# Chunk 1's products with wo held until chunk 0's third tile is normalized a second time, and the gate product put at a lower priority, in a planned adaLN, attention and MLP kernel

## The chip, the core and the metric

The kernel runs on one core of one Trainium2 chip. The metric is the device time of one execution in microseconds (us). Before the change the median of three runs is 2027.61 us (2023.54, 2027.61 and 2027.86).

## The reference

Input and output have 2048 rows of 512 numbers. The block is a conditioned attention layer followed by a mixer; `mod` gives three shifts and scales for each half, all of them rows of 512 numbers.

```python
sa, ca, ga, sb, cb, gb = split(silu(c) @ w_mod)
h = layernorm(x) * (1 + ca) + sa
x = x + ga * (attention(h; wqkv, 32 heads of 16) @ wo)
h = layernorm(x) * (1 + cb) + sb
# mixer B(h):
u  = gelu(layernorm(h) @ w1)                    # 512 -> 512
us = four column groups of u, shifted by +1, -1, +2, -2 rows
x1 = h + us @ w2                                # 512 -> 512
h2 = gelu(layernorm(x1) @ w3) @ w4              # 512 -> 1792 -> 512
out = x + gb * (x1 + h2)
```

So each row is normalized three times behind the attention: by the second adaLN layer norm, at the mixer's entry (the kernel's key `xn`), and after the product with w2 (key `xn4`). "Normalized for the second time" in this document means the last of these, `xn4`, the second of the two that the mixer makes.

## The kernel before

**Stages.** A prologue makes q, k and v. Then the attention runs over 4 chunks of 512 query rows and 16 pairs of heads. Behind the attention each chunk of 512 rows, four tiles of 128 rows, goes through what the code calls its tail. Chunk 0's tail begins during the last attention steps; those of chunks 1 to 3 begin when the attention is done. Every product in the tail is made of three TensorE matmuls (high by high, high by low, low by high, lines 356, 358 and 360), so that fp32 is kept.

**A chunk's tail.** `tail(ci)` transposes the attention's output of the chunk (`oT`, line 1244 of the helper `transposed`), and then, tile by tile, makes the product with wo (`wo_mm`). Each tile's product is followed by a chain of work on the other engines: VectorE adds it to x (line 1402), takes the statistics (lines 367, 368 and 1350, in the helper `ln_ops`), centres (1411), scales and shifts (1414) and takes the statistics again; GpSimd makes the inverse root (line 1353, and 1357 and 1358 for the shift); ScalarE applies the normalization (`xn`, line 1364). Two tiles at a time are then transposed by TensorE (`norm_T`, line 1244), split into high and low parts by ScalarE and VectorE (lines 350 and 346, tile name A), and multiplied with w1; the gelu takes ScalarE, VectorE and GpSimd (lines 1452 to 1456). Then comes the product with w2, tile by tile, with its own chain: VectorE adds (line 1507) and takes statistics, GpSimd and ScalarE normalize (`xn4`), and two more steps form the part of the output that does not go through w3: VectorE multiplies by 2 gb in place (line 1512, "the product with the gate") and GpSimd adds it into x1 (line 1513), after which the mark `("z", t)` is set. Chunk 0's w2 stage covers three tiles (its fourth needs rows of chunk 1), and the transposes of `xn4` of the three stand in one group.

**The rest of a chunk.** `rest(ci)` then makes the products with w3, the gelu and the products with w4, in seven pairs of 256 columns for chunk 0. Its weights are split on the way for chunk 0: a DMA brings a raw half (tile name raw), for w4 GpSimd multiplies it by the gate (line 1207), ScalarE makes the high part (1208), VectorE the low part (1209), and a DMA stores the split piece (Ws) for the later chunks. All other weights come back from Ws through a ring of buffers (DMA wr<-Ws, issued by SyncE at line 132); a buffer is loaded again only when the product that used it has been issued.

**What sets the order.** The order of the instructions on each engine is fixed when the program is built, by a planner (`Sched`). TensorE's work comes from generators. A generator yields a condition or a cost; `one()` goes through the list of generators and advances the first whose condition holds. Work on VectorE, ScalarE and GpSimd is put into chains (`sch.chain`), each a list of (engine, planned cost, function) with a ready time and a priority, 1 unless it is given. `misc` emits the chain step that can start first by the planner's clocks; among steps that could start at the same planned time, the chain that stands first in the list wins, and the list is sorted by priority, low numbers first. A step without an engine (None) is run by the planner itself, such as a mark.

Of the kernel before, what the change touches and what calls it, by code (L numbers as in the profile page):

```python
# [71 lines left out]
LNPC = 1  # L72
W0G = 1
WSPL = 1
NLOW = 1
CLOW = 1150
OUTW = 7000.0
# [241 lines left out]
def cD(n=CH):  # L319
    return n / 0.96 + 69  # L320


def cG(n=CH):
    return 2.2 * n + 40
# [3 lines left out]
def kernel(ctx, tc, A_x, A_wqkv, A_wo, B_w1, B_w2, B_w3, B_w4, c, w_mod, out):  # L328
# [951 lines left out]
    def tail(ci):  # L1280
# [91 lines left out]
        def normed(key, t, rs):  # L1372
            tag = xtag(key, t)
            xlive[tag] = xlive.get(tag, 0) + 1
            x = xn[key, t] = (tp if tag == "x4" else fa).tile([P, D], F32, name="xn", tag=tag, bufs=XN[tag])
            y = xbt[t]
            return ln_apply(x, y, rs), mark((key, t))
# [6 lines left out]
        def xn_room(key, t):  # L1384
            return xlive.get(xtag(key, t), 0) < XN[xtag(key, t)]
# [6 lines left out]
            xlive[xtag(key, ts[0])] -= len(ts)  # L1392

        for i, t in enumerate(new):
            yield lambda: sch.room() and xn_room("xn", t) and t in x1t and sch.now() >= arr.get(("x1", t), 0.0) and (ci < 2 or ("z", t - 2 * TPC) in done)
            yield from wo_mm(i, range(KT))
            b = banks.pop(i)
            x1 = x1t[t]
            xb = xbt[t] = pool_of(ci).tile([P, D], F32, name="xb", tag="xb", bufs=XBF if pool_of(ci) is fa else XBT)

            def x1_add(x1=x1, b=b):
                dve.tensor_tensor(x1, x1, b, op=OP.add)
                sch.free(b)

            r, m, ops = ln_ops(x1, True)
            r2, ops2 = ln_ops(xb)

            def center(xb=xb, x1=x1, m=m, ops=ops):
                ops[0][2]()
                sch.late = sch.put("G", 464, sch.T["D"] - cD() + XX, ops[1][2]) + XX  # L1410
                dve.scalar_tensor_tensor(xb, x1, m[:, 0:1], cbrow, op0=OP.subtract, op1=OP.mult)

            def scale(xb=xb, r=r):
                dve.scalar_tensor_tensor(xb, xb, r[:, 0:1], sbrow, op0=OP.mult, op1=OP.add)

            go = partial(sch.chain, ("D", cD(), x1_add), ("D", 2 * cD() + 150, center), ("D", cD(), scale), *ops2,
                         *normed("xn", t, r2), bank=b)
            go()
            if i % 2:
                spawn(norm_T(grp[i // 2], "xn", i // 2), ("T", ci, i // 2))  # L1420
# [77 lines left out]
        for si, ts in enumerate(sub):  # L1498
            yield lambda: all(("g", ci, i, n) in done for i in range(1 + (t0 + 1 in ts)) for n in range(4))
            for t in ts:  # L1500
                yield lambda: sch.room() and xn_room("xn4", t)
                b = dbank("w2")
                yield from rows_mm(b, lambda k, p: g[:, k, p, 130 + (t - t0) * P - SH[k]:][:, :P], w, range(KT), KT)
                xb, x1 = xbt[t], x1t[t]

                def xb_add(xb=xb, b=b):
                    dve.tensor_tensor(xb, xb, b, op=OP.add)
                    sch.free(b)

                r, ops = ln_ops(xb)  # L1510
                sch.chain(("D", cD(), xb_add), *ops, *normed("xn4", t, r),
                          ("D", cD(), lambda xb=xb: dve.scalar_tensor_tensor(xb, xb, 2.0, gbrow, op0=OP.mult, op1=OP.mult)),
                          ("G", cG(), lambda xb=xb, x1=x1: pool.tensor_tensor(x1, x1, xb, op=OP.add)),
                          mark(("z", t)), bank=b)
            spawn(norm_T(ts, "xn4", si), ("T4", ci, si))
        more()
        done.add(("w2", ci))
# [209 lines left out]
```

## Time and profile before

| what | value |
|---|---|
| median of the three runs | 2027.61 us |
| the profiled execution's own time | 2030.02 us |
| span of the profiled execution, first to last instruction | 2028.2 us |
| mean granted TensorE clock | 0.987 |
| first w2 product of chunk 0 | at 1550.15 us of the span |

A row of the profile's windows gives a stretch of the span, its length, the busy time of each engine in it (with the number of instructions), the mean clock that TensorE was granted, the busy share of the DMA engines and the bytes moved. A row of the timeline gives start, duration, engine, source line, operation, what is written from what, and a count where several instructions are merged; a bracket behind it tells how long the engine had been idle and which instruction ended that. All times are of one execution and count from the span's start. Lines are those of the kernel before.

### The profile page before, as it was taken

The page shows a single profiled execution, that of the slowest core. Times are in us where ns is not written, and L with a number is a line of the kernel's source. Part 1 is how long each engine was busy: PE and PEld are TensorE (multiplying, and loading weights), DVE is VectorE, ACT ScalarE, POOL GpSimd, SP SyncE. Part 2 cuts the span into 40 slices and gives each one's busy share as a digit, 9 for nine tenths or more (in the row PEclk, how much of TensorE's full clock was granted, in tenths as well). Part 3 has the DMA queues.
Part 4 walks back from the last instruction along what each step waited for, and adds up shares of the span by engine and source line. Part 5 has one row for each costly group of instructions (what it writes and reads, how often), then busy time and mean ns, then how long its engine had stood idle before and what let it go on. Part 6 is the DMA issues. An engine that isn't in the chain of part 4 may idle for free.

```text
span 2028.2 us, 41674 instructions
## 1 busy us (share of the span) xinstructions
PE 1941.1 (96%) x14456; PEld 1168.8 (58%) x14456; DVE 1658.8 (82%) x2979; ACT 1511.4 (75%) x3085; POOL 1569.9 (77%) x1488
## 2 busy tenths in 40 slices
PE   8999999999999999999999999999998889999999
PEld 5755554554444444444444444444447778898998
DVE  6398788879999999999999999999965786556443
ACT  6438887768999989999999999999984554344443
POOL 6349998879999999999999999999994554335222
PEclk9989999999999999999999999999999899999999
DMA  8877666544443435353434343454414677553541
GB/s 302 233 203 183 158 190 165 135 126 118 81 97 81 97 72 106 72 107 72 107 72 98 80 102 76 95 162 93 90 38 146 228 261 274 218 201 122 200 154 68
DMA packets 185508, 278.01 MB, mean 137 GB/s; under 512 B 117104, under 2 KB 127856, under 8 KB 169008
## 3 DMA queue, kind: packets, MB, share of 16 engines
q1 hardware_dynamic: 181792, 267.20, 49.0%
q10 hardware_dynamic: 2304, 4.20, 0.6%
q0 software_dynamic: 1200, 3.93, 0.5%
q8 instruction: 115, 1.88, 0.4%
q14 instruction: 97, 0.79, 0.1%
HBM read 211.81 MB, written 62.91 MB: 135 GB/s over the span
## 4 chain that ended last, share of the span: by engine, by line
PE 61%; DVE 16%; ACT 10%; issue 6%; POOL 4%; DMA 3%; SPq 1%; ACTq 0%; POOLq 0%; DVEq 0%
PE mb L993 13%; DVE mx L989 11%; PE pv L1083 9%; PE sc L1009 8%; ACT pt L1005 7%; PE w L360 6%; PE w L356 6%; PE w L358 6%; PE pv L1080 4%; PE ot L1110 3%; POOL pt L1058 2%; PE xT L1244 1%; DMA wr<-Ws 1%; DMA wst<-in_A_wqkv_dram 1%; SPq L132 1%
## 5 line engine op out<-in xcount | busy, mean ns | idle before, releaser
L989 DVE TENSOR_REDUCE mx<-mb 128x1 f32<-128x512 f32 x2048 | 1250.1, 680 | 74.5 <-PE mb L993 68.6
L1058 POOL TENSOR_SCALAR pt<-pt 128x1024 f16<-128x1024 uint16 x953 | 1248.1, 1365 | 78.7 <-ACT pt L1005 75.7
L1005 ACT ACTIVATE pt<-sc 128x512 int32<-128x512 f32 x2048 | 1061.3, 615 | 125.6 <-PE mb L993 98.0
L993 PE MATMUL mb<-kst,qtl 62*128 62x512 f32 x2048 | 782.7, 462 | 19.9 <-ACT pt L1005 9.9
L1009 PE MATMUL sc<-qtl,kst 64*128 64x512 f32 x2048 | 739.7, 449 | 5.0 <-DVE mx L989 2.5
L993 PEld LDWEIGHTS mb<-kst,qtl 62*128 62x128 f32 x2048 | 360.1, 193 | 232.3 <-ACT pt L1005 159.9
L1009 PEld LDWEIGHTS sc<-qtl,kst 64*128 64x128 f32 x2048 | 337.0, 186 | 186.8 <-DVE mx L989 119.3
L1083 PE MATMUL pv<-pt,vst 128*32 128x512 f16 x4096 | 385.3, 397 | 20.5 <-ACT ac L1100 20.5
L1456 POOL TENSOR_TENSOR g<-sq,g 128x256 fp32r<-128x256 f32 (+1 forms) x124 | 97.2, 787 | 200.6 <-ACT g L1455 187.2
L1080 PE MATMUL pv<-pt,vst 128*32 128x512 f16 (+1 forms) x2048 | 220.8, 389 | 2.5 <-POOL pt L1058 2.4
L1083 PEld LDWEIGHTS <-vst 128*32 128x32 bf16 x4096 | 91.8, 93 | 227.7 <-issue 209.2
L358 PE MATMUL w<-A,wr 128*128 128x256 f32 (+1 forms) x520 | 156.1, 300 | 0.3 <-DVE A L346 0.3
L356 PE MATMUL w<-A,wr 128*128 128x256 f32 (+1 forms) x520 | 155.9, 300 | 0.2 <-ACT A L350 0.2
L360 PE MATMUL w<-A,wr 128*128 128x256 f32 (+1 forms) x520 | 155.8, 300 | 0.0
L1452 ACT ACTIVATE sq<-w 128x256 f32<-128x256 f32 (+1 forms) x130 | 52.3, 402 | 136.0 <-PE w L360 127.2
L356 PE MATMUL w<-wr,g 128*128 128x512 f32 x270 | 106.9, 396 | 2.9 <-DMA wr<-Ws 2.9
L360 PE MATMUL w<-wr,g 128*128 128x512 f32 x270 | 106.5, 394 | 0.9 <-POOL g L1456 0.9
L358 PE MATMUL w<-wr,g 128*128 128x512 f32 x270 | 106.1, 393 | 0.0
L1434 DVE SCALAR_TENSOR_TENSOR sq<-sq,w 128x256 f32<-128x256 f32 (+1 forms) x130 | 58.3, 449 | 57.7 <-ACT sq L1454 57.5
L356 PEld LDWEIGHTS w<-A,wr 128*128 128x128 f32 x520 | 101.7, 196 | 1.6 <-ACT A L350 0.5
L358 PEld LDWEIGHTS w<-A,wr 128*128 128x128 f32 x520 | 101.5, 195 | 1.5 <-DVE A L346 0.5
L360 PEld LDWEIGHTS w<-A,wr 128*128 128x128 f32 x520 | 101.3, 195 | 0.5 <-issue 0.5
(156 smaller groups left out, 2128.5 us busy)
## 6 DMA issues: line engine op xcount, KB each, us to landing
wr<-Ws SPq DMA_DIRECT2D x66, 1024.0 KB, 5.5
vst<-Vs SPq DMA_DIRECT2D x64, 768.0 KB, 5.6
kst<-Ks SPq DMA_DIRECT2D x126, 384.0 KB, 6.2
Ws<-wr SPq DMA_DIRECT2D x14, 1024.0 KB, 6.2
qtl<-Qs SPq DMA_DIRECT2D x128, 96.0 KB, 4.3
Vs<-vt SPq DMA_DIRECT2D x32, 384.0 KB, 4.2
Ks<-qk SPq DMA_DIRECT2D x16, 512.0 KB, 4.2
Qs<-qk SPq DMA_DIRECT2D x16, 512.0 KB, 3.0
```

Source lines behind the costliest of these rows:

```text
L356: te.matmul(o, lh, rh, start=first, stop=False)
L358: te.matmul(o, lh, rl, start=False, stop=False)
L360: te.matmul(o, ll, rh, start=False, stop=last)
L989: end = sch.crit("D", 605, e + PX, lambda: dve.reduce_max(mxs[u][:, j, g, c:c + 1], b, axis=AX.X))
L993: return ready, lambda: te.matmul(b, lhs, kst[u % 3][r, c * CH:(c + 1) * CH], start=True, stop=True), after
L1005: ea = sch.crit("A", 480, e + PX, lambda: act.activation(pt[s][:, j], b, AF.Exp))
L1009: return ready, lambda: te.matmul(b, kst[u % 3][r, kt * P:(kt + 1) * P], qst[u][r], start=True, stop=True), after
L1058: e_low[s] = XP["G"] + sch.crit("G", 1345, ready, lambda: pool.tensor_scalar(o, i, 0.5, 1.0, op0=OP.mult, op1=OP.mult))
L1080: te.matmul(acc[r:r + n, :], v[:, kt + i, c:c + n].bitcast(F16), pt[s + i].bitcast(F16)[:, j, 0::2], start=False, stop=kt == NKT - 2, skip ...
L1083: te.matmul(acc[r:r + 32, :], v[:, kt, r:r + 32], pt[s].bitcast(F16)[:, j, 1::2], start=kt == 0, stop=False, skip_group_check=True)
L1110: te.matmul(b[:, t * n:(t + 1) * n], ac[:, t * P:(t + 1) * P], smat.rearrange("p j d -> p (j d)"), start=True, stop=True)
L1456: ("G", cG(n), lambda: pool.tensor_tensor(lo, sq, hi, op=OP.subtract)), (None, 0, end), bank=b)
```

## The change

Three constants are added, and three places are edited. `HOLD` is 0 and `i < 0` never holds, so for chunk 1 each of the four products with wo waits until the planner has set the mark `("xn4", 2)`, which stands behind the last step of the third tile's second normalization. `NPRIO` is 1, which is the priority that the chain had. The two steps of the gate are no longer at the end of the w2 chain: they become a chain of their own, put into the list when the normalization is planned as done, with priority 2 and without a bank of PSUM. The arithmetic is the same.

```diff
+ZPRIO = 2
+NPRIO = 1
+HOLD = 0
...
         for i, t in enumerate(new):
+            yield lambda: ci != 1 or i < HOLD or ("xn4", 2) in done
             yield lambda: sch.room() and xn_room("xn", t) and t in x1t and ...
             yield from wo_mm(i, range(KT))
...
                 r, ops = ln_ops(xb)
+                z = (("D", cD(), lambda xb=xb: dve.scalar_tensor_tensor(xb, xb, 2.0, gbrow, op0=OP.mult, op1=OP.mult)),
+                     ("G", cG(), lambda xb=xb, x1=x1: pool.tensor_tensor(x1, x1, xb, op=OP.add)), mark(("z", t)))
                 sch.chain(("D", cD(), xb_add), *ops, *normed("xn4", t, r),
-                          ("D", cD(), lambda xb=xb: dve.scalar_tensor_tensor(xb, xb, 2.0, gbrow, op0=OP.mult, op1=OP.mult)),
-                          ("G", cG(), lambda xb=xb, x1=x1: pool.tensor_tensor(x1, x1, xb, op=OP.add)),
-                          mark(("z", t)), bank=b)
+                          (None, 0, lambda z=z: sch.chain(*z, prio=ZPRIO)), bank=b, prio=NPRIO)
```

In the changed program every line from 75 on stands three further down, and from the held loop on four further down (1402 becomes 1406, 1507 becomes 1511), except that the gate's two steps, 1512 and 1513, become 1515 and 1516. TensorE, VectorE and GpSimd execute the same matmuls and element-wise steps in another order between chunk 0's first product with w2 and the transposes of chunk 1's second normalization; from those on, TensorE's list is the same in both.

TensorE, at chunk 0's first product with w2 (w_24911 is the PSUM bank of tile 0's w2 product, g the gelu's output). Before, nine of its twelve matmuls are followed by chunk 1's products with wo:

```order
L356 MATMUL w_24911<-wr,g_24623 128x512
L358 MATMUL w_24911<-wr,g_24623 128x512
L360 MATMUL w_24911<-wr,g_24623 128x512
L356 MATMUL wo<-wr,A 128x512
L358 MATMUL wo<-wr,A 128x512
L360 MATMUL wo<-wr,A 128x512
```

Three tiles of wo stand there, 36 matmuls, and then the remaining 27 of w2, with the transposes of chunk 1's first two tiles in between. In the changed program the 36 matmuls of w2 stand in one piece, and at their end (w_24957 is the third tile's bank) TensorE's list reads:

```order
L359 MATMUL w_24957<-wr,g_24623 128x512
L361 MATMUL w_24957<-wr,g_24623 128x512
L363 MATMUL w_24957<-wr,g_24623 128x512
L1247 MATMUL xT<-ident,xn 128x128 x12
L359 MATMUL wo<-wr,A 128x512
L361 MATMUL wo<-wr,A 128x512
L363 MATMUL wo<-wr,A 128x512
```

So the twelve transposes of chunk 0's three tiles now stand directly behind the third tile's product, and three tiles of wo behind them; these are followed by 27 matmuls of w3 and then the transposes of chunk 1's first two tiles.

VectorE, from the split of chunk 1's attention output on (A). Before, chunk 1's chain takes the next place, with the first w2 tile's addition 15 rows on:

```order
L346 TENSOR_TENSOR A<-xT,A 128x2x256 x4
L1402 TENSOR_TENSOR x_24869<-x_24869,wo 128x512
L367 BN_STATS tst<-x_24869 128x6
L368 BN_AGGR tmv<-tst 128x2
L1350 TENSOR_SCALAR tmv<-tmv 128x1
L1411 SCALAR_TENSOR_TENSOR xb<-x_24869,tmv,cbrow 128x512
L1414 SCALAR_TENSOR_TENSOR xb<-xb,trs,sbrow 128x512
L1402 TENSOR_TENSOR x_24871<-x_24871,wo 128x512
```

In the changed program the three w2 tiles come first there. L1511 is a w2 tile's addition and L1515 the product with the gate; the rows from tile 1's addition (w_24932) to tile 2's statistics are:

```order
L1511 TENSOR_TENSOR xb<-xb,w_24932 128x512
L370 BN_STATS tst<-xb 128x6
L371 BN_AGGR tmv<-tst 128x2
L1353 TENSOR_SCALAR tmv<-tmv 128x1
L1515 SCALAR_TENSOR_TENSOR xb<-xb,gbrow 128x512
L1511 TENSOR_TENSOR xb<-xb,w_24957 128x512
L370 BN_STATS tst<-xb 128x6
L371 BN_AGGR tmv<-tst 128x2
L1353 TENSOR_SCALAR tmv<-tmv 128x1
```

The first tile's product with the gate thus still stands ahead of the third tile's addition. Then come the other two products with the gate, the low parts of four raw halves and the split of the transposes, and only then chunk 1's first addition (L1406). Further on, chunk 1's second tile (x_24871) goes through these rows on VectorE in the changed program:

```order
L1406 TENSOR_TENSOR x_24871<-x_24871,wo 128x512
L1418 SCALAR_TENSOR_TENSOR xb<-xb,trs,sbrow 128x512
L370 BN_STATS tst<-xb 128x6
L371 BN_AGGR tmv<-tst 128x2
L1353 TENSOR_SCALAR tmv<-tmv 128x1
L370 BN_STATS tst<-x_24871 128x6
L371 BN_AGGR tmv<-tst 128x2
L1353 TENSOR_SCALAR tmv<-tmv 128x1
L1415 SCALAR_TENSOR_TENSOR xb<-x_24871,tmv,cbrow 128x512
L1406 TENSOR_TENSOR x_24873<-x_24873,wo 128x512
L1418 SCALAR_TENSOR_TENSOR xb<-xb,trs,sbrow 128x512
L370 BN_STATS tst<-xb 128x6
```

Its last statistics are now eleven rows behind its addition, with no row of chunk 0 in between.

## The prediction

> **What bounds the kernel now.** I read the page's first part first, then the windows over the stretch that the change reorders, then TensorE's waits there, then the timeline of each engine around those waits.
>
> ```profile
> span 2028.2 us, 41674 instructions
> PE 1941.1 (96%) x14456; PEld 1168.8 (58%) x14456; DVE 1658.8 (82%) x2979; ACT 1511.4 (75%) x3085; POOL 1569.9 (77%) x1488
> ```
>
> TensorE (PE) is busy 96% of the span, so a reordering can only gain what TensorE loses: time in which it has nothing to do, and time at a lower clock. TensorE's list differs from chunk 0's first w2 matmul, at 1550.15 us, to the sixteen transposes of chunk 1's second normalization, at 1677.87. The windows cut this stretch at its waits:
>
> ```profile
> core 0: us, PE busy (x) PEld busy (x) DVE busy (x) ACT busy (x) POOL busy (x), PEclk, DMA share, GB/s
> 1550.15:1677.87 127.72, 110.31 (x567) 97.47 (x565) 103.93 (x190) 61.21 (x122) 71.33 (x92) 0.93 0.63 224
> 1567.00:1590.00 23.00, 13.38 (x75) 11.75 (x73) 19.73 (x41) 11.79 (x21) 14.24 (x25) 0.84 0.61 221
> 1590.00:1639.00 49.00, 46.97 (x260) 42.13 (x260) 37.66 (x73) 24.36 (x52) 27.43 (x37) 0.97 0.62 220
> 1639.00:1651.00 12.00, 6.36 (x25) 5.93 (x25) 10.52 (x17) 6.60 (x13) 9.30 (x10) 0.72 0.61 228
> 1677.87:2028.00 350.13, 341.32 (x2055) 306.80 (x2052) 187.38 (x387) 143.78 (x347) 123.89 (x186) 1.00 0.48 174
> ```
>
> TensorE's idle time in the stretch is 127.72 - 110.31 = 17.4 us. The lower clock costs (1 - 0.84) x 13.38 + (1 - 0.97) x 46.97 + (1 - 0.72) x 6.36 = 2.1 + 1.4 + 1.8 = 5.3 us. So 22.7 us are lost, 1.1% of the span, and 105.0 us are work that stays. Behind the stretch the list does not change, and its 8.8 us of idle stay. VectorE is busy for 103.9 of the 127.7 us, so a shorter stretch leaves it little slack. What ended TensorE's waits in the stretch:
>
> ```profile
> PE xT L1244 <- ACT xn L1364: 15.3, 5, 5.6
> PE w L356 <- DMA wr<-Ws: 2.0, 1, 2.0
> ```
>
> The waits are transposes that wait for ScalarE's normalized tiles, and one load of weights. Here are the transposes that waited, with two matmuls that show the pace behind the third wait:
>
> ```profile
> 1568.89 0.99 PE L1244 MATMUL xT<-ident,xn 128*128 128x128 f32 x7 [1.57 <-ACT xn L1364]
> ...
> 1579.36 2.39 PE L1244 MATMUL xT<-ident,xn 128*128 128x128 f32 x10 [5.58 <-ACT xn L1364]
> ...
> 1589.06 1.57 PE L1244 MATMUL xT<-ident,xn 128*128 128x128 f32 x7 [2.22 <-ACT xn L1364]
> ...
> 1591.07 0.41 PE L358 MATMUL w<-A,wr 128*128 128x256 f32 x1
> 1591.28 0.41 PE L360 MATMUL w<-A,wr 128*128 128x256 f32 x1
> ...
> 1645.59 1.75 PE L1244 MATMUL xT<-ident,xn 128*128 128x128 f32 x7 [5.64 <-ACT xn L1364]
> ```
>
> A wait costs more than itself when the clock falls behind it. Behind the 2.22 us wait two matmuls that are 256 wide start 0.21 us apart; at full clock matmuls twice as wide start 0.23 apart (1611.25 and 1611.48, below). Behind the 1.57 us wait seven transposes take 0.99 us, 0.14 each; behind 5.58, 2.22 and 5.64 they take 0.24, 0.22 and 0.25 each. So the 5.3 us of lost clock belong to these three waits, about 2 us for a long one.
>
> **The change, part by part.** Nothing is added or removed on any engine; the terms are the waits in the new order.
>
> *Removed: the 1.57, 5.58 and 2.22 us waits.* Their transposes move, and with them the clock that followed, 2.1 + 1.4 us.
>
> *First new wait: chunk 0's third tile.* The 36 matmuls of w2 now run in one piece. How VectorE and ScalarE are occupied ahead of the third tile, two rows tell, and how long its normalization takes, the same chain of chunk 1's third w2 tile:
>
> ```profile
> 1552.60 2.57 DVE L346 TENSOR_TENSOR A<-xT,A 128x512 fp32r<-128x512 f32 x4
> ...
> 1570.51 2.19 ACT L1208 ACTIVATE wr<-raw 128x512 fp32r<-128x512 f32 x4
> ...
> 1611.25 0.39 PE L358 MATMUL w<-wr,g 128*128 128x512 f32 x1
> 1611.48 0.39 PE L360 MATMUL w<-wr,g 128*128 128x512 f32 x1
> ...
> 1611.91 0.69 DVE L1507 TENSOR_TENSOR xb<-xb,w 128x512 f32<-128x512 f32 x1
> ...
> 1615.29 0.82 ACT L1364 ACTIVATE xn<-xb,trs 128x512 f32<-128x512 f32 x1 [1.08 <-POOL trs L1358]
> ```
>
> At 0.23 us from start to start the last w2 matmul starts at 1550.15 + 35 x 0.23 = 1558.2 and ends 0.39 later, at 1558.6. From addition to normalized tile it is 1616.1 - 1611.9 = 4.2 us. VectorE splits A until 1555.2; then tile 0 is normalized at 1559.4, and its product with the gate, in the order still ahead of tile 2's addition, reads and overwrites the same tile, so it waits for that. Tile 2's addition starts at 1560.0 and its tile is ready at 1560.0 + 4.2 = 1564.2. ScalarE's four weight halves (2.2 us) stand between tiles 1 and 2 and end at about 1563.5, so they just fit. TensorE waits 1564.2 - 1558.6, about 5.5 us, and the clock costs 2 us behind it. The wo products behind the transposes then cover the split of A. The cover that this wait had before, 36 matmuls of wo, is what the change takes away. Bounds: 4.2 us without the gate's detour, 7 if one more chain gets ahead.
>
> *Second new wait: chunk 1's first two tiles.* From the second tile's product to their transposes TensorE has 12 matmuls of wo (2.7 us) and 27 of w3 (384 wide, so three quarters of 0.23 each: 4.7), 7.4 us. On VectorE the twelve rows shown with the change stand in the way; their groups:
>
> ```profile
> L1209 DVE TENSOR_TENSOR wr<-raw,wr 128x512 fp32r<-128x512 f32 x26 | 25.0, 990 | 0.0
> ...
> L367 DVE BATCH_NORM_STATS2 tst<-xb 128x6 f32<-128x512 f32 x13 | 8.9, 687 | 0.1
> L1434 DVE SCALAR_TENSOR_TENSOR sq<-sq,w 128x384 f32<-128x384 f32 x12 | 6.6, 549 | 3.7 <-ACT sq L1454 3.5
> ...
> L1414 DVE SCALAR_TENSOR_TENSOR xb<-xb,trs,sbrow 128x512 f32<-128x512 f32 x6 | 5.4, 902 | 0.9 <-POOL trs L1353 0.9
> ...
> L1402 DVE TENSOR_TENSOR x<-x,wo 128x512 f32<-128x512 f32 x6 | 4.1, 680 | 0.8 <-PE wo L360 0.8
> ```
>
> Two additions (0.68), two scalings (0.90), three statistics (0.69, with their two small steps about 1.0) and one centring (about an addition) make 6.9 us. Behind them stand the root on GpSimd and the normalization: the 4.2 us of the chain above less its addition and statistics, 2.5 us. 9.4 - 7.4 = 2.0 us. Bounds: 0, and 2.2 with 1.4 of clock, as the nearest such wait had. I take 2.0 without clock.
>
> *Third new wait: chunk 1's last two tiles.* Between the fourth tile's product and its transposes lie 21 matmuls of w4, 24 of w3 and 31 of w1: 4.8 + 4.1 + 3.6 = 12.5 us. From the split of the first two tiles on, VectorE's order holds seven steps of gelu (3.8 at 0.55), five weight halves (5.0 at 0.99), four additions (2.7), two sets of statistics (2.0), and two scalings, a centring and two splits (3.9), 17.4 us. With the terms so far TensorE ends the first two tiles' transposes at about 1582 and stands at the last two's at about 1601. VectorE starts that split at about 1584, since ScalarE has three weight halves ahead of it, and ends at 1601.4; the tile is ready 2.5 us later, near 1604. I take 3.0, with 0.8 of clock; bounds 0 and 5.64 with 2.4, the wait of the same kind at 1645.59.
>
> *Weights.* The second w2 piece loads when w1's first half is done. From the chain of waits:
>
> ```profile
> 1598.07 6.55 DMA wr<-Ws
> 1604.66 0.50 PE w L356
> ```
>
> From issue to use it took 6.6 us. In the new order 24 matmuls of w1 (0.12 each, half of 0.23) and 6 of w2 cover 2.9 + 1.4 = 4.3, so the wait is 2.3 where it was 2.0. The loads of w1's and w2's first pieces are issued later too, behind the last wo, but 11 us or more ahead of their use. SyncE has weight stores ahead of them; these end with the same wo product, so I cost that at nothing; if one of these loads landed late, it would show as a second DMA wait.
>
> *Fourth wait: chunk 2's first two tiles, 5.64 us before.* The last products with wo are followed by nine more w3 matmuls than before (10 instead of 1 in the third w3 pair), 1.6 us. VectorE also has fewer weight halves left there, since pairs 0 and 1 come earlier. I take 1.5, bounds 0 and 5.64; no clock.
>
> *The gate's priority elsewhere.* In chunks 1 to 3 the gate's product moves by a few rows behind the statistics of the next tile. The transposes of those tiles come much later than their normalization (at 1677.87 for chunk 1), so the cost is nothing; the gap to them covers it.
>
> **Sum.** New loss: idle 5.5 + 2.0 + 3.0 + 2.3 + 1.5 = 14.3, clock 2.0 + 0.8 = 2.8, together 17.1 us, against 22.7: 5.6 us less. The profiled execution took 2030.02 us around its span of 2028.2, so its like would take 2024.4. It is 2.4 above the median of the runs, 2027.61; from that, 2022.0 us.
>
> The Trainium skill (TensorE: Matmul & The Clock Gate, section "HAM oscillation — how this bites in real kernels") gives the rule "no PE-idle gaps >~3.4µs", and half the clock for about 3.4 us behind such a gap. That speaks against one gap of 5.5 us and for several short ones. By it the two long waits of before would cost 1.7 us each and only the first new one would, so the gain would be (17.4 + 3.4) - (14.3 + 1.7) = 4.8 us. The trace disagrees on the threshold, since the half pace also followed the 2.22 us wait.
>
> **Rivals.**
> - *All the later waits are covered* (0.12). Only the first one and the weights are left: 5.5 + 2.0 + 2.3 = 9.8, a gain of 12.9, 2014.7 us. For it speaks that 36 wo matmuls and the w3 pairs now lie between chains; against it VectorE's 104 us of work.
> - *The loss only moves* (0.26). The wait at the third tile takes the place of 5.58 us, and the late chains of chunk 1 that of 5.64 us: if the third and fourth wait come to 5 and 4 us, with 2 of clock in one of them, the loss is 5.5 + 2 + 2 + 5 + 2 + 2.3 + 4 = 22.8: 2027.7 us. For it: VectorE is busy for 86 to 88% of the two windows in which TensorE waits longest. Against it: the chain that TensorE waits for first now stands together on VectorE, without another chunk's rows in it.
> - *VectorE's queue becomes the bound* (0.16). Holding wo moves all of chunk 1's additions behind the w2 tiles, among gelu steps and weight halves. If two of the second to fourth waits are like 1645.59 (5.64 + 2.4), the loss is 7.5 + 2.3 + 16.1 + 2.0 = 27.9: 5.2 us slower, 2032.8. Against it: 36 matmuls of wo and the first w3 pairs lie between. It decides from 12.9 us over these three waits on (22.7 - 9.8); I expect 7.3.
>
> **How the numbers follow.** The forecast has 0.46. About 0.2% (4 us) is what a measurement of this kernel can tell from no change. Faster by more: 0.46 + 0.12 = 0.58; within: 0.26; slower: 0.16. The range from 2014 to 2032 takes in the first rival's time and the bounds of the waits, and leaves out most of the last rival.
>
> **What would show it.** Right: in the changed profile TensorE waits once for 5 to 6 us behind w2's third tile for ScalarE, with slow matmuls of wo behind it; the wait ahead of chunk 2's transposes shrinks to under 3 us; and from chunk 1's second normalization on all starts are earlier by the gain. Wrong: waits of 5 us at chunk 1's transposes, a second wait for a load of weights, or a start of the unchanged part that does not move.

## The result, and the profile after

| | before | changed |
|---|---|---|
| median of 12 runs | 2026.53 us | 2019.37 us |
| range | 2023.54 to 2029.34 | 2016.26 to 2022.31 |
| profiled execution, span | 2030.02, 2028.2 us | 2021.44, 2019.7 us |

The ratio is 0.9966 with a 95% interval of 0.9956 to 0.9975: 7.2 us, or 0.34%, faster. The forecast was 2022.0 with a range from 2014 to 2032.

The stretch that the change reorders, from chunk 0's first w2 matmul to the sixteen transposes of chunk 1's second normalization, took 127.6 us before: the prediction ends it at 1677.87, but the transposes start at 1677.71. These are the windows of the changed kernel over the stretch, the piece behind the first waits in which TensorE never stops, and the part behind the stretch (us, then busy time of TensorE, its weight loads, VectorE, ScalarE and GpSimd with their instructions, then TensorE's clock, DMA share and GB/s):

```profile
1549.47:1670.78 121.31, 107.62 (x566) 94.33 (x564) 100.97 (x190) 60.24 (x123) 71.66 (x92) 0.97 0.66 236
1563.87:1570.12 6.25, 6.25 (x20) 5.36 (x21) 3.79 (x6) 2.60 (x5) 3.30 (x3) 0.52 0.98 371
1670.78:2019.70 348.92, 339.84 (x2055) 305.55 (x2053) 187.82 (x387) 143.11 (x347) 125.49 (x186) 1.00 0.47 175
```

And one of the kernel before, behind its stretch:

```profile
1714.00:1720.00 6.00, 5.63 (x35) 5.64 (x36) 3.35 (x7) 3.77 (x10) 0.67 (x2) 0.72 0.02 7
```

The stretch is 6.3 us shorter. TensorE is idle in it for 121.31 - 107.62 = 13.7 us (17.4 before), and its busy time is 2.6 us above the prediction's 105.0 us of work (5.3 before). All of the lower clock lies behind the first waits, (1 - 0.52) x 6.25 = 3.0 us; from there to the end of the stretch the clock is 1.00. That is more than 2.6, because the prediction multiplied the mean clock of windows in which TensorE is partly idle with its busy time, and the mean counts the idle time too. Read in windows of half a microsecond, the lower clock costs 5.8 us before and 3.0 us now, and the work is about 104.5 us. Of the span's 8.5 us the remaining 2.2 lie ahead of the stretch and behind it, where TensorE's list is the same in both; 1.6 of them lie behind it and are busy time, since before the clock fell there once more (0.72 in the window at 1714 us).

TensorE's waits in the stretch, by what ended them (us in all, how many, the longest):

```profile
PE xT L1247 <- ACT xn L1367: 10.5, 6, 2.9
PE w L363 <- POOL g L1460: 2.2, 1, 2.2
PE w L359 <- DMA wr<-Ws: 0.9, 1, 0.9
```

And one by one in TensorE's timeline, with the first three waits at chunk 0's three tiles, the pace of wo behind them, then chunk 1's first two tiles, its last two, the weights, a gelu, and chunk 2's first two tiles:

```profile
1558.70 0.33 PE L1247 MATMUL xT<-ident,xn 128*128 128x128 f32 x1 [0.56 <-ACT xn L1367]
1560.60 0.33 PE L1247 MATMUL xT<-ident,xn 128*128 128x128 f32 x1 [1.57 <-ACT xn L1367]
1563.87 2.40 PE L1247 MATMUL xT<-ident,xn 128*128 128x128 f32 x10 [2.94 <-ACT xn L1367]
...
1567.35 0.63 PE L359 MATMUL wo<-wr,A 128*128 128x512 f32 x1
1567.77 0.63 PE L361 MATMUL wo<-wr,A 128*128 128x512 f32 x1
...
1570.12 0.40 PE L361 MATMUL wo<-wr,A 128*128 128x512 f32 x1
1570.35 0.39 PE L363 MATMUL wo<-wr,A 128*128 128x512 f32 x1
...
1582.53 0.98 PE L1247 MATMUL xT<-ident,xn 128*128 128x128 f32 x7 [1.54 <-ACT xn L1367]
1605.38 0.98 PE L1247 MATMUL xT<-ident,xn 128*128 128x128 f32 x7 [2.52 <-ACT xn L1367]
1617.82 0.50 PE L359 MATMUL w<-wr,g 128*128 128x512 f32 x1 [0.94 <-DMA wr<-Ws]
1652.70 0.50 PE L363 MATMUL w<-wr,g 128*128 128x512 f32 x1 [2.23 <-POOL g L1460]
1659.21 0.98 PE L1247 MATMUL xT<-ident,xn 128*128 128x128 f32 x7 [1.40 <-ACT xn L1367]
```

Three waits with 5.07 us in all stand at chunk 0's tiles. Behind them matmuls of wo start 0.42 us apart, and from 1570.12 on 0.23 apart. No other wait is followed by a slow pace: seven transposes take 0.98 us behind 1.54, 2.52 and 1.40 us, where before they took up to 1.75. The unchanged part starts 6.9 us earlier in the span (1670.78 instead of 1677.71).

One wait is new in kind, the 2.23 us at 1652.70 for the low part of a gelu on GpSimd. GpSimd's timeline around it, with VectorE's step that GpSimd waited for:

```profile
1650.68 0.99 POOL L1356 TENSOR_TENSOR trs<-tmv,mhalf 128x1 f32<-128x1 f32 x1 [6.38 <-DVE tmv L1353]
1651.64 1.00 POOL L1460 TENSOR_TENSOR g<-sq,g 128x384 fp32r<-128x384 f32 x1
...
1650.45 0.15 DVE L1353 TENSOR_SCALAR tmv<-tmv 128x1 f32<-128x1 f32 x1
```

The low part stands in GpSimd's queue behind the root of chunk 2's second tile, and that root waits 6.38 us for its statistics.

### The profile page after: what moved, and what is told of

The parts are those of the page before. It is cut to its first block, busy times and chain, and to the rows that moved or that the text cites. A ratio compares the mean times of both kernels' runs of the same rounds, so it can differ in the third digit from the quotient of the medians.

```text
span 2019.7 us, 41655 instructions
## 1 busy us (share of the span) xinstructions
PE 1934.4 (96%) x14456; PEld 1162.1 (58%) x14456; DVE 1656.3 (82%) x2979; ACT 1510.2 (75%) x3085; POOL 1571.9 (78%) x1488
## 4 chain that ended last, share of the span: by engine, by line
PE 61%; DVE 16%; ACT 9%; issue 6%; POOL 4%; DMA 3%; SPq 0%; ACTq 0%; POOLq 0%; DVEq 0%
PE mb L996 13%; DVE mx L992 12%; PE pv L1086 9%; PE sc L1012 8%; ACT pt L1008 7%; PE w L363 5%; PE w L359 5%; PE w L361 5%; PE pv L1083 4%; PE ot L1113 3%; POOL pt L1061 2%; PE xT L1247 1%; POOL trs L1356 1%; PE v L359 1%; DMA wr<-Ws 1%
## 5 line engine op out<-in xcount | busy, mean ns | idle before, releaser
L361 PE MATMUL w<-A,wr 128*128 128x256 f32 (+1 forms) x520 | 153.4, 295 | 0.3 <-DVE A L349 0.3
L359 PE MATMUL w<-A,wr 128*128 128x256 f32 (+1 forms) x520 | 153.2, 295 | 0.3 <-ACT A L353 0.3
L363 PE MATMUL w<-A,wr 128*128 128x256 f32 (+1 forms) x520 | 153.1, 294 | 0.0
L359 PEld LDWEIGHTS w<-A,wr 128*128 128x128 f32 x520 | 98.7, 190 | 1.7 <-ACT A L353 0.5
L361 PEld LDWEIGHTS w<-A,wr 128*128 128x128 f32 x520 | 98.7, 190 | 1.6 <-DVE A L349 0.5
L363 PEld LDWEIGHTS w<-A,wr 128*128 128x128 f32 x520 | 98.6, 190 | 0.5 <-issue 0.5
```

Of the source, the lines that this page charges most:

```text
L359: te.matmul(o, lh, rh, start=first, stop=False)
L361: te.matmul(o, lh, rl, start=False, stop=False)
L363: te.matmul(o, ll, rh, start=False, stop=last)
```

## The experiments

The **theory**: the gain comes from chains that stand together on VectorE, so that the long waits of before (5.58 and 5.64 us) become one long wait, in three pieces, and several short ones, and only the long one costs the pace. It needs both parts of the change. **Rivals**: one part alone does it; the clock differs by chance from execution to execution; or VectorE has no slack, and what is won at one wait comes back at another.

All edits are to the changed kernel. Added lines shift the line numbers in their profiles. "Stretch" is the same stretch in the one profiled execution; "above" is TensorE's busy time above 105.0 us, the fill taken off (4.09 us for 36, as in a row below); with about 104.5 us of work it is some 0.4 us too low in most rows. Each ratio is to the kernel before, run on the same chip; rows come from four chips, so they are compared by their ratios.

| run | edit | stretch | idle | above | median | ratio (95%) |
|---|---|---|---|---|---|---|
| e5 | none | 120.23 | 12.6 | 2.6 | 2018.95 | 0.9957 (0.9945 to 0.9970) |
| e1 | hold alone | 131.36 | 18.3 | 8.1 | 2028.79 | 1.0010 (0.9997 to 1.0023) |
| e2 | priority alone | 127.35 | 16.6 | 5.7 | 2026.63 | 0.9999 (0.9988 to 1.0011) |
| e3 | fill, twice | 118.82 | 8.7 | 1.0 | 2024.23 | 0.9983 (0.9968 to 0.9997) |
| e6 | fill, once | 118.43 | 8.4 | 1.0 | 2020.01 | 0.9968 (0.9957 to 0.9979) |
| e4 | released earlier | 121.73 | 13.7 | 3.0 | 2022.28 | 0.9979 (0.9966 to 0.9991) |
| e7 | two holds | 130.11 | 16.6 | 8.5 | 2030.56 | 1.0018 (1.0008 to 1.0027) |
| e8 | two holds, at w2 | 131.95 | 19.3 | 7.6 | 2031.85 | 1.0022 (1.0010 to 1.0033) |
| e9 | gate behind | 119.98 | 12.9 | 2.0 | 2019.33 | 0.9973 (0.9962 to 0.9984) |
| e10 | root behind | 124.70 | 14.6 | 5.2 | 2023.82 | 0.9990 (0.9980 to 1.0001) |
| e11 | e9, e10 and fill | 121.90 | 10.4 | 3.1 | 2023.46 | 0.9983 (0.9972 to 0.9995) |
| e12 | all rows behind, fill | 119.85 | 10.2 | 1.0 | 2020.70 | 0.9979 (0.9966 to 0.9992) |

### The changed kernel again (e5)

> The changed kernel once more, on the chip and beside the runs that the next three are compared with. Theory (the gain is in the order, so it comes again): 2019 to 2020 us beside 2026 to 2027 of before, the stretch from the first w2 matmul to the sixteen transposes again 121.3 us. Rival (the gain was one of the clock drops that differ from execution to execution): a stretch that differs by 3 us or more, and a time nearer to before.

The gain came again, 8.5 us by the medians, so it isn't one of the clock's chance drops. The stretch was 120.23 us, 1.1 less than in the first profile, with the same waits in the same places but for the 0.56 us. So one profile each can't tell apart two stretches that differ by about 1 us.

### Each part alone (e1, e2)

For e1 the gate's two steps go back to the end of the chain; for e2 the line with the hold is taken out.

```diff
 sch.chain(("D", cD(), xb_add), *ops, *normed("xn4", t, r),
-          (None, 0, lambda z=z: sch.chain(*z, prio=ZPRIO)), bank=b, prio=NPRIO)
+          ("D", cD(), lambda xb=xb: dve.scalar_tensor_tensor(xb, xb, 2.0, gbrow, op0=OP.mult, op1=OP.mult)),
+          ("G", cG(), lambda xb=xb, x1=x1: pool.tensor_tensor(x1, x1, xb, op=OP.add)),
+          mark(("z", t)), bank=b, prio=NPRIO)
```

```diff
-yield lambda: ci != 1 or i < HOLD or ("xn4", 2) in done
```

> The hold alone, with the gate's two steps back at the end of each w2 chain. Theory (both parts count): on VectorE tile 0's gate product now stands ahead of tile 1's statistics and waits for tile 0's normalized tile, and three weight halves (2.7 us) stand ahead of tile 2's statistics. So tile 2 is normalized about 3.6 us later than in the changed kernel (at about 1567.4 instead of 1563.8), TensorE's wait at the third tile grows from 5.1 to about 8.5 us, and half of the gain of 7.2 us is lost: about 2023 us. Rival A (the hold does all of it, the gate's priority nothing): 2019.4 us as the changed kernel, third-tile wait 5 us. Rival B (the gate's priority does all of it): 2026.5 us as before.

> The gate's lower priority alone, without the hold; TensorE again puts 36 wo matmuls between the w2 tiles. Theory: the waits of before stay, because what made them long is chunk 1's chain between the w2 tiles on VectorE: waits for normalized tiles of 12 to 16 us in the stretch, 2025 to 2027 us in all (before: 15.3 and 2026.5). Rival (the gate's priority does most of it): 2019 to 2021 us and waits of about 10 us.

The timeline with the hold alone: TensorE's waits at chunk 0's tiles and at chunk 2's, and on VectorE the first tile's product with the gate, which now stands ahead of the second tile's statistics:

```profile
1562.80 0.47 PE L1247 MATMUL xT<-ident,xn 128*128 128x128 f32 x1 [4.10 <-ACT xn L1367]
1565.91 2.40 PE L1247 MATMUL xT<-ident,xn 128*128 128x128 f32 x10 [2.64 <-ACT xn L1367]
...
1663.64 1.76 PE L1247 MATMUL xT<-ident,xn 128*128 128x128 f32 x7 [3.60 <-ACT xn L1367]
...
1558.35 0.69 DVE L1516 SCALAR_TENSOR_TENSOR xb<-xb,gbrow 128x512 f32<-128x512 f32 x1 [1.46 <-ACT xn L1367]
```

Its windows over the stretch and at chunk 2's transposes:

```profile
1549.44:1680.80 131.36, 113.08 (x566) 98.79 (x565) 102.80 (x192) 60.99 (x124) 72.22 (x92) 0.91 0.66 227
1663.00:1671.00 8.00, 7.36 (x28) 6.88 (x29) 6.22 (x10) 3.98 (x8) 3.46 (x3) 0.60 0.77 240
```

With the priority alone, the wait at chunk 0's last tiles in the timeline:

```profile
1574.38 2.39 PE L1247 MATMUL xT<-ident,xn 128*128 128x128 f32 x10 [5.58 <-ACT xn L1367]
```

The priority alone keeps the 5.58 us wait to the hundredth and gains nothing in time, as expected. But all waits for normalized tiles sum to 10.8 us, where 12 to 16 were expected: the one at chunk 2's tiles is 2.06 us instead of 5.64. Ahead of these, TensorE now waits 2.31 and 0.93 us for parts of gelus, and the clock falls behind these and behind 2.33 us for weights. The hold alone isn't half the gain but none: the waits at chunk 0's tiles are 7.0 us (8.5 expected), but busy time above the work rises to 8.1 us. The clock falls not only behind these but also behind 3.19 us at chunk 1's last two tiles, behind 2.15 us for weights and at chunk 2's tiles, where the wait is long again (3.60). Rival A falls with e1; rival B, whose time e1 has, falls with e2. Neither part is worth anything alone here. At chunk 0's tiles the rows say why: with the gate's product ahead of the next tile's statistics, VectorE waits 1.46 us for ScalarE in the middle of the chains that the hold has put together. Why the later waits grow again in e1 isn't shown.

### Useless work in the long wait (e3, e6)

The transposes of the identity go into the PSUM bank that the real ones then overwrite. This is e6; e3 lacked the condition on `filled`.

```diff
+NFILL = 36
 b = dbank("xT")
+if n > 2 * P and kk[0] == 0 and not filled:
+    filled.append(1)
+    for _ in range(NFILL):
+        te.transpose(b[:, :P], ident, ident)
```

> The changed kernel with 36 transposes of the identity put ahead of the twelve transposes of chunk 0's three normalized tiles, into the bank that these then overwrite; all other lists are unchanged. The work is useless; it only keeps TensorE busy for 36 x 0.14 = 5.0 us in its wait of 5.1 us. Theory (the slow matmuls behind the wait cost 2.8 to 3.0 us and come from TensorE having been idle): the transposes and the wo matmuls behind run at full pace, wo starts 0.23 us apart, the stretch is 2 to 3 us shorter, 2016.5 to 2017.5 us. Rival A (the slow pace has another cause, or useless transposes don't keep the clock): the same 2019.4 us, or later by up to 0.5 us because the real transposes now queue behind the fill. Rival B (VectorE holds the rest: the 2 to 3 us come back as a longer wait at chunk 1's first two tiles, 1.5 now, 3.5 to 4.5 then): 2019.4 us with a shorter first half.

> As the fill before, but with the 36 useless transposes only at chunk 0's three tiles; the first try issued them a second time in the last chunk, where nothing waits (39 more rows, 4 us). Theory: the profile of the first try had 2.5 us less in the stretch (118.8 instead of 121.3), so without the second fill 2016.5 to 2017.5 us. Rival (the clock that is kept here is lost elsewhere, or the fill costs as much as it keeps): 2019.4 us as the changed kernel.

e3 issued the fill once more in chunk 3, where nothing waits; that row of its timeline, and then e6's windows over the stretch, the wait and a piece behind chunk 1's first two tiles, with the transposes there:

```profile
1906.69 4.09 PE L1248 MATMUL xT<-ident 128*128 128x128 f32 x36
```

```profile
1551.16:1669.59 118.43, 110.08 (x601) 97.53 (x600) 100.36 (x190) 60.12 (x122) 71.36 (x92) 0.99 0.68 245
1560.00:1572.00 12.00, 10.83 (x72) 9.60 (x71) 11.05 (x20) 5.99 (x11) 7.92 (x10) 1.00 0.61 221
1582.05:1585.55 3.50, 3.50 (x15) 3.50 (x14) 3.43 (x8) 3.29 (x8) 2.01 (x2) 0.51 0.00 0
```

```profile
1581.55 1.22 PE L1254 MATMUL xT<-ident,xn 128*128 128x128 f32 x7 [1.89 <-ACT xn L1374]
```

The clock behind the wait is 1.00 where it was 0.52, and in both runs the stretch is 1.4 to 2.9 us shorter than in the two profiles without a fill. So the slow pace behind the first waits does come from TensorE's idling, and it cost 3.0 us. But in both runs the clock then falls behind chunk 1's first two tiles, where it had stayed at 1.00 in the changed kernel: (1 - 0.51) x 3.50 = 1.7 us, behind a wait of only 1.89 us. e6's rival, that the clock kept here is lost elsewhere, held in part. In the total the fill shows no gain (0.9968 against 0.9957 and 0.9966, with intervals that overlap), and both runs miss the 2016.5 to 2017.5 us of their theory; e3 also pays for its second fill.

### Released one tile earlier (e4), and a second hold (e7, e8)

The added lines are those of e4, e7 and e8 in this order:

```diff
-yield lambda: ci != 1 or i < HOLD or ("xn4", 2) in done
+yield lambda: ci != 1 or i < HOLD or ("xn4", 1) in done
+yield lambda: ci != 1 or (("xn4", 1) in done if i < 2 else ("xn", grp[0][1]) in done)
+yield lambda: ci != 1 or (("w2", 0) in done if i < 2 else ("xn", grp[0][1]) in done)
```

> The hold is released one tile earlier, when the second tile's normalization is planned; VectorE's order through the three w2 tiles stays as in the changed kernel, and 12 wo matmuls (2.8 us) now stand in the third-tile wait; 48 w3 matmuls instead of 27 then stand ahead of chunk 1's first two tiles. Theory (the third-tile wait is a real loss that any work can fill): that wait falls from 5.1 to about 2.3 us, the wait at chunk 1's first two tiles from 1.5 to about 0, and the time to about 2015 to 2016 us. Rival (VectorE, 84% busy in the stretch, is the bound, and a wait filled here only comes back later): waits of 13 to 14 us in the stretch as now, 2018 to 2020 us.

With twelve wo matmuls in it, the wait at chunk 0's third tile fell to 2.46 us, as expected. But e4's timeline has a second wait behind it, at chunk 1's first two tiles; below it are GpSimd's rows ahead of that wait:

```profile
1560.24 2.40 PE L1247 MATMUL xT<-ident,xn 128*128 128x128 f32 x10 [2.46 <-ACT xn L1367]
...
1583.69 1.75 PE L1247 MATMUL xT<-ident,xn 128*128 128x128 f32 x7 [6.66 <-ACT xn L1367]
...
1578.62 0.99 POOL L1356 TENSOR_TENSOR trs<-tmv,mhalf 128x1 f32<-128x1 f32 x1 [3.12 <-DVE tmv L1353]
1579.58 1.34 POOL L1210 TENSOR_TENSOR raw<-raw,gbrow 128x512 f32<-128x512 f32 x1
1580.89 0.99 POOL L1356 TENSOR_TENSOR trs<-tmv,mhalf 128x1 f32<-128x1 f32 x1
...
1576.92 0.15 DVE L1353 TENSOR_SCALAR tmv<-tmv 128x1 f32<-128x1 f32 x1
```

The second tile's statistics are ready at 1577.07, but its root stands on GpSimd behind the third tile's, which waits until 1578.6, and behind a raw half, and starts at 1580.89. The stretch and the sum of the waits are as in the changed kernel, as the rival said; the median is above its 2018 to 2020 us. e7 and e8 take the third tile out of the way.

> Chunk 1's first two wo tiles are released one tile earlier (as in the run with the earlier release), and its last two are held until its second tile is normalized. Theory (the 6.7 us wait of the earlier release came from GpSimd's queue: the second tile's root stood behind the third tile's root, which waited for statistics on VectorE): with the third tile out of the way that wait falls to 2 us or less, the third-tile wait of chunk 0 stays at 2.5, and the time is 2014 to 2016 us. Rival (VectorE is the bound; gelu steps and weight halves take the third tile's place and the wait stays at 5 us or more): 2018 to 2021 us.

> As the run before it, but the first two wo tiles are released as soon as chunk 0's last w2 product is issued, so that 16 wo matmuls (3.7 us) stand in the third-tile wait instead of 12. Theory: that wait falls from 5.1 to about 1.4 us with no slow matmuls behind it, the others as in the run before: 2012 to 2015 us. Rival (chunk 1's additions now get ahead of chunk 0's third tile or its split, or VectorE is the bound): waits of 12 us or more in the stretch, 2018 to 2021 us.

e7's timeline has TensorE at a w4 product instead, waiting for its weights, and on GpSimd the raw halves of these weights behind the roots, with the second tile's root behind them:

```profile
1581.67 0.80 PE L361 MATMUL w<-wr,g 128*128 128x512 f32 x1 [5.06 <-ACT wr L1213]
...
1576.18 0.99 POOL L1358 TENSOR_TENSOR trs<-tmv,mhalf 128x1 f32<-128x1 f32 x1 [5.11 <-DVE tmv L1355]
...
1578.19 0.99 POOL L1358 TENSOR_TENSOR trs<-tmv,mhalf 128x1 f32<-128x1 f32 x1
...
1579.68 2.50 POOL L1212 TENSOR_TENSOR raw<-raw,gbrow 128x512 f32<-128x512 f32 x2
...
1583.57 0.99 POOL L1358 TENSOR_TENSOR trs<-tmv,mhalf 128x1 f32<-128x1 f32 x1
```

With w4 now ahead of chunk 1's first two tiles, w4's weights are late by 5.06 us (4.90 in e8). The wait at the two tiles is 1.36 us, but only because TensorE comes to them later: their transposes start 37.5 us after the first w2 matmul, as in e4 (37.6). The second tile's root no longer stands behind the third's, but behind the two raw halves and a gelu's low part: its statistics are ready at 1581.31, and it starts at 1583.57. So these runs don't show that the third tile's root alone made the wait in e4. In e8 the wait at chunk 0's third tile fell to 1.61 us with the transposes at full pace, as expected, but chunk 2's tiles then wait 5.56 us. Both kernels are slower than before, which neither the theories nor the rivals had. What stands behind a root on GpSimd in these rows waits for VectorE's statistics with it.

### The rows between the third tile and its normalization (e9, e12)

In e9 tile 0's product with the gate is emitted behind the third tile's addition; VectorE's list differs in one pair of rows, the others in none. The first diff is e9's, where the gate's steps of tile 0 are kept in `late`. In e12 (the second diff, without the halves) all that stood in the way goes behind: on VectorE the gate's products of tiles 0 and 1, on GpSimd tile 0's addition into x1, on ScalarE four weight halves; 32 transposes fill the wait.

```diff
 def xb_add(xb=xb, b=b, t=t):
     dve.tensor_tensor(xb, xb, b, op=OP.add)
     sch.free(b)
+    if t == 2:
+        while late:
+            late.pop(0)()
+        done.add(("a", 2))
```

```diff
+if (ci, t) == (0, 2):
+    def root(fn=ops[1][2]):
+        fn()
+        done.add("root2")
+        while late:
+            late.pop(0)()
+    ops = ops[0], (*ops[1][:2], root)
+def gate(fn):
+    if ci or "root2" in done:
+        fn()
+    else:
+        late.append(fn)
...
```

> The changed kernel with one pair of rows exchanged on VectorE and nothing else moved on any engine: tile 0's product with the gate now stands behind the third tile's addition instead of ahead of it. Theory: the third tile's addition no longer waits for tile 0's normalization and the gate product (0.9 us in the changed kernel: free at 1558.35, started at 1559.29), so the third tile comes 0.9 us earlier, TensorE's three waits at the tiles sum to 4.1 to 4.2 us instead of 5.1, and the stretch is 0.9 us shorter; in all 2018 to 2018.5 us, which the total alone can't tell from the changed kernel. Rival A: ScalarE's four weight halves, which end at 1562.6, now hold the third tile, and the wait stays at 4.8 us or more. Rival B: the 0.9 us come back at chunk 1's first two tiles (1.5 us becomes 2.4), and the stretch stays at 120.2 to 121.3 us.

> The changed kernel with what stands between the third tile's addition and its normalized tile put behind it: on VectorE the gate products of tiles 0 and 1 (behind the third tile's statistics), on GpSimd the addition of tile 0 into x1 (behind the third tile's root), on ScalarE the four weight halves (behind the third tile's normalization); and 32 useless transposes of the identity (0.11 us each in the run with one fill, 3.5 us) in the wait. Nothing else moves. Theory: addition at 8.7 us from the first w2 matmul, statistics until 10.3, root until 11.5, normalized at 12.4, so that the transposes that wait for the third tile start at 12.4 to 12.6 us instead of 13.9 to 14.4; with the pace kept, the stretch is 1.5 us shorter than with the fill alone (118.4): 116.5 to 117.5 us, and 2015 to 2018 us in all. Rival A (one of the moved rows doesn't matter and another row or the root's own duration holds the tile): the third tile at 13.5 us or later. Rival B (the third tile comes earlier, but chunk 1's tiles on VectorE don't): the waits at chunk 1's tiles grow by the 1.5 us, from 1.9 to 3.4 at the first two, and the stretch stays at 118 us or more.

e9's rows of VectorE, GpSimd and ScalarE for the third tile, from its addition to its normalization:

```profile
1557.17 0.69 DVE L1512 TENSOR_TENSOR xb<-xb,w 128x512 f32<-128x512 f32 x1 [0.18 <-PE w L363]
1557.77 0.69 DVE L1526 SCALAR_TENSOR_TENSOR xb<-xb,gbrow 128x512 f32<-128x512 f32 x1
1558.37 0.69 DVE L370 BATCH_NORM_STATS2 tst<-xb 128x6 f32<-128x512 f32 x1
...
1558.54 1.27 POOL L1527 TENSOR_TENSOR x<-x,xb 128x512 f32<-128x512 f32 x1
1559.77 1.00 POOL L1356 TENSOR_TENSOR trs<-tmv,mhalf 128x1 f32<-128x1 f32 x1
...
1561.66 0.82 ACT L1367 ACTIVATE xn<-xb,trs 128x512 f32<-128x512 f32 x1 [0.23 <-POOL trs L1361]
```

The gate's product only slid between addition and statistics, and the root waits behind a GpSimd addition of 1.27 us. The three waits sum to 4.74 us, no less than e5's 4.51: nearly rival A's 4.8, though GpSimd and not ScalarE holds the tile. In e12, with all three out of the way, the third tile comes 13.0 us after the first w2 matmul (13.9 to 14.4 without the change, 12.4 expected). These are e12's waits there and at chunk 1's first two tiles:

```profile
1560.92 1.31 PE L1264 MATMUL xT<-ident,xn 128*128 128x128 f32 x10 [0.60 <-ACT xn L1384]
1577.68 0.33 PE L1264 MATMUL xT<-ident,xn 128*128 128x128 f32 x1 [2.56 <-ACT xn L1384]
1579.90 1.44 PE L1264 MATMUL xT<-ident,xn 128*128 128x128 f32 x7 [1.89 <-ACT xn L1384]
```

The time won comes back at chunk 1's first two tiles, 4.45 us where the fill alone had 1.89. Rival B held, and the stretch is longer than e6's by 1.4 us. The median, 2020.70 us, misses the theory's 2015 to 2018.

### The new wait on GpSimd (e10), and three edits together (e11)

In e10 the root of chunk 2's second tile is emitted behind the gelu's low part; GpSimd's list differs in one pair of rows. e11 joins e9, e10 and 30 filling transposes.

```diff
-sch.late = sch.put("G", 464, sch.T["D"] - cD() + XX, ops[1][2]) + XX
+sch.late = sch.put("G", 464, sch.T["D"] - cD() + XX, partial(held.append, ops[1][2]) if (ci, i) == (2, 1) else ops[1][2]) + XX
...
+def low():
+    pool.tensor_tensor(lo, sq, hi, op=OP.subtract)
+    free_held()
```

> The changed kernel with one pair of rows exchanged on GpSimd and nothing else moved: the root of chunk 2's second tile, which waits until 1650.45 for its statistics, now stands behind the low part of a gelu, which had its input at 1646.7 and stood behind it. Theory (the wait of 2.2 us for the gelu's low part comes from the order of GpSimd's queue alone): that wait is gone. What is then late is VectorE, which is busy without a gap from 1643 to 1661 in the changed kernel and sets chunk 2's first two tiles; their wait grows from 1.4 to 3 to 3.6 us, with slow transposes behind it, and the stretch is shorter by 0.5 us at most: 2018.5 to 2019.5 us. Rival A (nothing else is late): the stretch is 2.2 us shorter, 2016.8 us. Rival B (the low part was late for another reason): the wait for it stays at 2 us or more.

> Both exchanges and 30 useless transposes (4.1 us) in the third-tile wait, otherwise as the changed kernel. Theory (the three add up: 0.9 from the gate, 2 to 2.5 of clock from the fill, 0 to 0.5 from GpSimd's exchange): a stretch of 116.5 to 118 us and 2015.5 to 2017 us. Rival (VectorE has no slack: what is won at the third tile comes back at chunk 1's tiles): a stretch of 119 us or more, 2018 to 2019.5 us.

The wait for the low part is gone, so its cause was the order of GpSimd's queue. What e10's timeline has in its place, with the low part and the weight halves beside it on VectorE, and the same halves in the changed kernel:

```profile
1660.10 0.33 PE L1247 MATMUL xT<-ident,xn 128*128 128x128 f32 x1 [0.98 <-ACT xn L1373]
1663.71 1.75 PE L1247 MATMUL xT<-ident,xn 128*128 128x128 f32 x7 [3.28 <-ACT xn L1373]
...
1650.67 1.51 POOL L1449 TENSOR_TENSOR g<-sq,g 128x384 fp32r<-128x384 f32 x1 [2.46 <-ACT g L1470]
1650.61 2.11 DVE L1212 TENSOR_TENSOR wr<-raw,wr 128x512 fp32r<-128x512 f32 x2
```

```profile
1646.70 1.28 DVE L1212 TENSOR_TENSOR wr<-raw,wr 128x512 fp32r<-128x512 f32 x2
```

TensorE came to chunk 2's tiles sooner, VectorE didn't: from the same addition to the same statistics it took 7.5 us instead of 6.6, because the halves took 2.11 instead of 1.28 us beside GpSimd's low part. Two waits of 2.23 and 1.40 us at full pace became 0.98 and 3.28 us with slow transposes behind. The theory had the place and the 3 to 3.6 us right and the sum wrong: the stretch is 3.4 to 4.5 us longer than in the changed kernel, not shorter by 0 to 0.5, and by the medians e10 gains 2.3 us on the kernel before, where the changed kernel gained 7.2 and 8.5. Not all of this belongs to the edit: in e10's profile the clock was also 0.50 from 1607.6 to 1611.0, behind the same 2.08 us wait at chunk 1's last two tiles that left it at 1.00 in e5. e11 has the same waits (0.93 and 3.28 us), which eat what the fill keeps; its rival held for the stretch, and its median, 2023.46 us, is above both ranges.

No version beats the changed kernel by more than can be measured. The medians of e4, e6, e11 and e12 are 2 to 3.5 us above what their stretches would give beside before's. In part the profiled executions aren't typical (before's took 3.5 us more than its median, e4's 3.9 less, e11's and e12's 1.8 and 2.3 less); the rest is open.

## Why the prediction was right

The forecast was 22.7 us of loss falling to 17.1; by the same reckoning the profiles show 16.3 and 15.2 (23.2 falling to 16.7 and 15.6 with the clock read in short windows). By its own steps:

- *First new wait, 5.5 us with 2 of clock.* Measured 5.07 (4.51 again in e5) and 3.0, so the clock term was set too low, as it was for the kernel before. The place, the chain and the slow wo matmuls were as described, though the wait came in three pieces. The bound "4.2 us without the gate's detour" was wrong: e9 took the gate out of the addition's way and nothing came of it, since the gate's product then stood ahead of the statistics and a GpSimd addition ahead of the root. Moving these and ScalarE's halves together (e12) brought the tile 0.9 to 1.4 us forward; what each is worth isn't shown.
- *Second, 2.0, and third, 3.0 with 0.8 of clock.* Measured 1.54, and 2.52 (2.08 in e5) at full pace.
- *Weights, 2.3.* Measured 0.94. The load was issued at 1612.66 and used at 1617.82, 5.2 us, where the row of before gave 6.6; the term was mis-sized by that. Why the load was faster isn't shown.

```profile
1612.66 0.34 SPq L135 DMA_DIRECT2D wr<-Ws  x1
```

- *Fourth, 1.5.* Measured 1.40, but not for the reason given. TensorE had lost 2.23 us just ahead, for the gelu, and came that much later to these tiles; where that wait was gone (e10), TensorE waited 0.98 and 3.28 us here. That the number fits is luck.
- *Not foreseen: 2.23 us on GpSimd.* The prediction followed VectorE's list and took GpSimd's steps for durations. The order of the roots on GpSimd, and what stands behind them, wasn't followed. The sum held (14.3 us of idle predicted, 13.7 measured) because the five foreseen waits were set too high by 2.8 us together, which is luck too.
- *Rivals.* "All the later waits are covered" and "the loss only moves" aren't what happened. "VectorE's queue becomes the bound" didn't happen in the changed kernel, but its mechanism is in the rows of e4, e7, e10 and e12: what was won at one wait was lost at the next. It sits a little elsewhere than the rival put it: in the changed kernel, e4 and e7 it is GpSimd's queue that passes VectorE's lateness on, to roots, raw halves and gelus.
- *The rest.* 6.3 of the 8.5 us between the two profiled spans lie in the stretch. The rest is ahead of it and behind it, where TensorE's list is the same; the medians give 7.2 and 8.5 us, the stretches 6.3 and 7.3. Of the stretch's 6.3 us, 3.7 are idle time and 2.5 busy time, which is the clock's.

The Trainium skill (TensorE: Matmul & The Clock Gate, section "HAM oscillation — how this bites in real kernels") would have the pace drop only behind gaps above about 3.4 us. The runs disagree: the longest gap at chunk 0's tiles is 2.94 us here and 2.46 in e4, and behind both ten transposes take 2.40 us instead of 1.31; in e6 the clock fell behind 1.89 us.

## What to carry to other kernels

When a reordering gains on an engine that waits, ask for each wait that goes away which queue is late next: here most of what was won at one more wait came back at a later one. A few short waits can be cheaper than one long one of the same sum, because the long one also takes the pace, so removing a short wait can cost time; but waits of about 2 us took the pace in some runs too, so look at the clock behind every wait and not only at the wait. Follow the in-order queue of a small helper engine as closely as those of the busy ones: a step of 1 us that waits for another engine holds up everything behind it.

## What the hardware showed

- The drop to half pace has no sharp bound in the length of a single wait: it followed waits of 1.89 us (e6), 2.08 us (e10), 2.22 us (before), 2.46 us (e4) and 2.94 us (changed kernel), and didn't follow 2.08 us (e5), 2.23 and 2.52 us (changed kernel). It can set in late: in e10 the seven transposes behind 2.08 us still took 0.98 us. Filling a wait with useless transposes kept the clock at 1.00 behind that wait, and the clock fell behind a later one in all four runs that did so (e3, e6, e11, e12).
- A drop to half pace lasted about 3.4 us (e6, e10) or twice that: behind the same 2.94 us wait the clock stood at 0.50 from 1563.0 to 1569.9 us in the changed kernel and from 1566.6 to 1570.1 in e10. One of 3.4 us with TensorE at work costs 1.7 us, so two profiles of the same order can differ by that much.
- Two VectorE subtractions of 128x512 took 2.11 us beside a GpSimd instruction that itself took 1.51, and 1.28 us without; the GpSimd step took 1.00 without them.
- The same instructions ahead of the stretch ended between 1545.05 us (e2) and 1553.05 us (e10) in the profiled executions. A difference of 2 us between kernels is therefore better read from the stretch than from the span, with the drops of the clock in it set apart.
